# Linear attention in chunks of 64 tokens of two batches, with its products in quarter and eighth parts of the TensorE array

## The chip, the cores and the metric

The kernel runs on one core of a Trainium2 chip. The metric is the device time of one execution in microseconds. The kernel before takes 512.79 us (median of 3 runs, 512.62 to 513.18).

## The reference

The program computes a linear attention with a decaying state and feeds its output, token by token, to a feed-forward layer with a cosine gate. Cut to what is computed:

```python
# r, k, v: (4 batches, 8 heads, 768 tokens, 48), w, u: (8, 48)
for t in range(S):
    cur = einsum('bhd,bhe->bhde', u * k[t], v[t])
    y[t] = einsum('bhd,bhde->bhe', r[t], state + cur)
    state = w[..., None] * state + einsum('bhd,bhe->bhde', k[t], v[t])
x = y.transpose(0, 2, 1, 3).reshape(3072, 384)
h = x @ w_in                      # (384, 2048)
out = (h * cos(h)) @ w_out        # (2048, 384)
```

The two weights are given in 64-bit floats, everything else in 32-bit floats; the output is float32.

## The kernel before, in words

**Attention** is cut into 24 chunks of 128 tokens of one batch (`chunk(i)`: batch `i % 4`, part `i // 4` of its 768 tokens). Within a chunk, k and r are brought into a form with the 48 entries of a head along the partitions (two heads, `j` = 0 and 1, at partitions 0 to 47 and 64 to 111; four such pairs `p`), scaled with the decay. Then four products follow on TensorE (PE), all in float32:

- the scores, `mm_a` (L819): k by r for 8 heads, 128x128 each. Head `j` uses one half of the array's rows and writes to a PSUM bank of its own;
- `mm_x` (L840): r by the state before the chunk (`zt`), 12 pieces of 32 output rows each, in four column parts of the array;
- `mm_x2` (L853): the masked scores `A` by v, 16 pieces of 32 output rows, added to the same bank;
- `mm_z` (L875): k by v, the chunk's own contribution to the state, 48x48 for each head.

Between them ScalarE (ACT) writes a diagonal matrix into `A` (L809, the term with u) and VectorE (DVE) copies the scores above the diagonal over it (L826, `copy_predicated`). After `mm_z` DVE adds the contribution to the state `zc` and multiplies by the decay (L932, L933; L930 for a batch's first chunk), and ACT spreads it to `zt` (L868). The result x is split into a high and a low part (L914 on ACT, L919 on DVE).

The first 12 chunks have k and r transposed on PE (L730). The other 12 ("late") load k and r in a staged form and have them transposed by DVE (L738) and scaled by GpSimd (POOL, L743).

**The feed-forward part** takes blocks of 3 chunks (384 tokens). A step is 9 matmuls for h (L316: high and low parts, three products of three slices), the gate on ACT and DVE (qi L327, rest L330, cos L333, gate L1030, gh L1033, gl L1036) and 9 matmuls for the output (L322). Weights come as 64-bit words (`raw`) and are turned into high and low parts on ACT, DVE and POOL.

**Order.** A planner in the program itself (`Plan`) takes every piece of work as an operation with an engine, a due time, a cost and the buffers that it needs, plays the program many times with changed due times, keeps the best order and emits the instructions in that order. Each engine then works through its own list in order. A buffer (`Buf`) is bound to a tile of a ring by the planner. The 8 PSUM banks are such tiles: three for the output sums (`B_ACC`), two or three for h, and three for late attention chunks (`B_ATT`: two for scores, then x, then state). All chunk loads are issued by SyncE (SP).

## Time and profile before

| | us |
|---|---|
| median of 3 runs | 512.79 |
| profiled execution, its own time | 512.26 |
| its span, first to last instruction | 510.5 |
| PE busy in the span | 501.5 (98%) |
| DVE, ACT, POOL busy | 381.0, 331.0, 177.1 |

A row of a group reads: line, engine, operation, output and inputs, shape, count; then busy time and the mean duration in ns of one; then idle time before it and what ended it. A timeline row is start, length, and then the instruction with the count of records that were merged. Busy time of PE is the union of overlapping records.

### The profile page before, as it was taken

What the parts mean: (1) busy time and instruction counts of PE and PEld (TensorE: products, weight loads), DVE (VectorE), ACT (ScalarE), POOL (GpSimd) and SP (SyncE); (2) the same over time, 40 slices, a digit from 0 to 9 for tenths busy, and PEclk for the clock granted to TensorE, in tenths of its full rate; (3) what the DMA queues carried; (4) which work ended last, traced back from release to release, by engine and by line L of the source; (5) the groups of instructions that cost most, each with busy time, mean ns of one, the idle gap of its engine ahead of it and who ended that gap; (6) DMA issues with size and microseconds to landing.
All of it is one profiled execution on the core that took longest, in us unless ns stands there. A gap on an engine that the chain in (4) does not pass through costs nothing.

```text
span 510.5 us, 11742 instructions
## 1 busy us (share of the span) xinstructions
PE 501.5 (98%) x4389; PEld 480.0 (94%) x4389; DVE 381.0 (75%) x773; ACT 331.0 (65%) x833; POOL 177.1 (35%) x184
## 2 busy tenths in 40 slices
PE   8999999999999999999999999999999999999995
PEld 5788899999999999999999999999999999999995
DVE  6898999888888875576777777777777767756553
ACT  2989987767667756556657465575665765655453
POOL 6777422445454451242426224224044041300000
PEclk9999999999999999999999999999999999999999
DMA  8999226586666593524676736446455465200001
GB/s 137 179 179 190 79 86 218 152 167 156 157 140 131 127 180 44 76 65 67 160 146 151 159 99 167 111 156 152 105 130 140 142 170 114 89 16 33 1 1 49
DMA packets 114975, 61.56 MB, mean 121 GB/s; under 512 B 78433, under 2 KB 110818, under 8 KB 114914
## 3 DMA queue, kind: packets, MB, share of 16 engines
q1 hardware_dynamic: 109586, 53.50, 42.7%
q0 software_dynamic: 5184, 7.08, 9.9%
q8 instruction: 35, 0.57, 0.5%
q14 instruction: 26, 0.21, 0.2%
q10 hardware_dynamic: 144, 0.20, 0.1%
HBM read 48.96 MB, written 11.80 MB: 119 GB/s over the span
## 4 chain that ended last, share of the span: by engine, by line
PE 94%; DMA 2%; DVE 1%; ACT 1%; issue 1%; POOL 0%; SPq 0%; DVEq 0%; POOLq 0%; ACTq 0%
PE bank L322 41%; PE bank L316 39%; PE bank L819 4%; PE bank L853 4%; PE bank L840 3%; PE bank L875 2%; PE bank L730 1%; DMA v<-in_v_dram 1%; DMA k<-in_k_dram 1%; ACT A L809 1%; PE bank L1094 0%; DVE pq L440 0%; POOL f L765 0%; DVE a L800 0%; DVE rq L447 0%
## 5 line engine op out<-in xcount | busy, mean ns | idle before, releaser
L322 PE MATMUL bank<-w_out_hi,gh 128*128 128x384 f32 x384 | 131.9, 344 | 0.0
L322 PE MATMUL bank<-w_out_hi,gl 128*128 128x384 f32 x384 | 129.8, 338 | 0.0
L316 PE MATMUL bank<-xh,w_in_lo 128*128 128x384 f32 x384 | 129.7, 338 | 0.0
L322 PE MATMUL bank<-w_out_lo,gh 128*128 128x384 f32 x384 | 129.5, 337 | 0.0
L316 PE MATMUL bank<-xh,w_in_hi 128*128 128x384 f32 x384 | 129.1, 336 | 0.0
L316 PE MATMUL bank<-xl,w_in_hi 128*128 128x384 f32 x384 | 128.8, 335 | 0.0
L330 DVE SCALAR_TENSOR_TENSOR f<-bank,qi 128x384 f32<-128x384 f32 (+1 forms) x132 | 71.4, 543 | 47.0 <-ACT qi L327 46.5
L327 ACT ACTIVATE qi<-bank 128x384 int32<-128x384 f32 (+1 forms) x132 | 62.8, 479 | 57.7 <-PE bank L316 57.0
L1033 ACT CAST gh<-f 128x384 fp32r<-128x384 f32 (+1 forms) x132 | 65.7, 500 | 48.9 <-DVE f L1030 46.9
L1030 DVE TENSOR_TENSOR f<-bank,f 128x384 f32<-128x384 f32 (+1 forms) x132 | 71.2, 542 | 32.5 <-ACT f L333 30.3
L1036 DVE TENSOR_TENSOR gl<-f,gh 128x384 fp32r<-128x384 f32 (+1 forms) x132 | 80.7, 613 | 19.6 <-ACT gh L1033 19.1
L333 ACT ACTIVATE f<-f 128x384 f32<-128x384 f32 (+1 forms) x132 | 67.3, 513 | 41.6 <-DVE f L330 40.8
L322 PEld LDWEIGHTS bank<-w_out_hi,gh 128*128 128x128 f32 x384 | 72.0, 188 | 3.0 <-issue 0.8
L316 PEld LDWEIGHTS bank<-xh,w_in_lo 128*128 128x128 f32 x384 | 72.2, 188 | 0.3 <-DVE w_in_lo L631 0.3
L316 PEld LDWEIGHTS bank<-xh,w_in_hi 128*128 128x128 f32 x384 | 72.2, 188 | 0.3 <-issue 0.2
L316 PEld LDWEIGHTS bank<-xl,w_in_hi 128*128 128x128 f32 x384 | 72.1, 188 | 0.0
L322 PEld LDWEIGHTS bank<-w_out_hi,gl 128*128 128x128 f32 x384 | 72.1, 188 | 0.0
L322 PEld LDWEIGHTS bank<-w_out_lo,gh 128*128 128x128 f32 x384 | 72.0, 188 | 0.0
L809 ACT ACTIVATE A<-ident,a 128x128 f32<-128x128 f32 x192 | 59.6, 391 | 4.9 <-DVE a L800 4.8
L743 POOL TENSOR_TENSOR kT<-kT,decT_k 112x512 f32<-112x512 f32 x12 | 15.6, 1301 | 129.3 <-DVE kT L738 74.4
L621 POOL TENSOR_TENSOR f<-f,raw 128x384 int32<-128x384 int32 x32 | 36.7, 1148 | 60.8 <-DVE f L610 31.7
L1078 POOL DMA_DIRECT2D out_dram<-f x36 | 32.7, 1012 | 40.6 <-DVE f L1030 17.2
(88 smaller groups left out, 589.5 us busy)
## 6 DMA issues: line engine op xcount, KB each, us to landing
raw<-in_moe_w_in_dram SPq DMA_DIRECT2D x32, 384.0 KB, 3.2
raw<-in_moe_w_out_dram SPq DMA_DIRECT2D x32, 384.0 KB, 3.2
out_dram<-f POOLq DMA_DIRECT2D x36, 192.0 KB, 4.5
k<-in_k_dram SPq DMA_DIRECT2D x24, 192.0 KB, 4.2
v<-in_v_dram SPq DMA_DIRECT2D x24, 192.0 KB, 5.1
raw<-in_k_dram SPq DMA_DIRECT2D x47, 96.0 KB, 3.1
raw<-in_r_dram SPq DMA_DIRECT2D x47, 96.0 KB, 2.1
out_dram<-f SPq DMA_DIRECT2D x23, 192.0 KB, 1.9
```

Of the source, the lines that this page charges most:

```text
L316: nc.tensor.matmul(ph, a, b_, start=(i == 0), stop=(i == len(mm) - 1))
L322: nc.tensor.matmul(acc, a[:, ts], b_[:, f, :], start=(first and i == 0), stop=(last and i == 2))
L327: nc.scalar.activation(qi, ph, AF.Copy, scale=INV_2PI, bias=0.25)
L330: nc.vector.scalar_tensor_tensor(q, ph, INV_2PI, qi, op0=ALU.mult, op1=ALU.subtract)
L333: nc.scalar.activation(q, q, AF.Sin, scale=TWO_PI, bias=0.5 * math.pi)
L621: lambda: nc.gpsimd.tensor_tensor(ai(), ai(), cn(), op=ALU.add),
L809: nc.scalar.activation(A[j]()[:, p, :], ident, AF.Copy, scale=ab()[:, h : h + 1])
L819: nc.tensor.matmul(cube(Ap[j])[:, p, :], kT()[ps, p, :], rT()[ps, p, :], start=True, stop=True)
L1030: nc.vector.tensor_tensor(g()[:, cs], ph()[:, cs], q()[:, cs], op=ALU.mult)
L1033: nc.scalar.copy(gh()[:, cs], g()[:, cs])
L1036: nc.vector.tensor_tensor(gl()[:, cs], g()[:, cs], f32(gh())[:, cs], op=ALU.subtract)
L1078: nc.gpsimd.dma_start(dst, ob(), accum_op=ALU.add)
```

## The change

A chunk is now 64 tokens of two batches (`m = i % 2` is the pair of batches, `c = i // 2` one of 12 parts): the first batch's tokens stand at partitions 0 to 63 of the natural layout, the other's at 64 to 127. There are still 24 chunks of 128 tokens, and blocks of the feed-forward part still have 3.

- Scores: 16 matmuls of 64x64 instead of 8 of 128x128; head `j` picks the rows, batch `b` the columns of the array. The square blocks between the two batches are no longer computed. `A`, the diagonals and the masks have 64 columns for each head instead of 128.
- State: 16 matmuls with 64 rows each, directly behind the scores in the same operation (the first two chunks have them apart); only a batch pair's last chunk has none, so 22 chunks have a state and 22 read one (20 and 20 before). `zc` and `zt` hold two batches.
- `mm_x`: 24 matmuls of 32x64 instead of 12 of 32x128. `mm_x2`: 32 matmuls of 32x64 with 64 rows instead of 16 of 32x128 with 128 rows, written so that eight in a row are in eight different parts of the array.
- PSUM: scores with state, and x, each take a pair of neighbouring banks, one bank for each half of the array's rows. The planner knows pairs (`parts`). Late chunks have one pair (banks 5 and 6) for both; h has three banks throughout.
- Each load of a chunk is two DMA issues of 64 partitions, and eight instead of four for the staged ones.

The core of the diff:

```diff
+        pair = [Tile(bank_all[:, i : i + 2], bank[i : i + 2]) for i in range(7)]
+        B_ACC, B_H, B_ATT = bank[0:3], bank[3:5] + bank[7:8], bank[5:8]
+        P_ATT = pair[5:6]
+        P_EARLY = [pair[5], pair[6], pair[3], pair[0]]
...
-            b, c = i % B, i // B
+            m, c = i % NM, i // NM
...
-            Ap = [Buf(bk) for _ in range(2)]
+            sp = Buf(bp)
-            xp = Buf(bk)
-            zp = Buf(bk)
+            xp = Buf(bp)
+            half = [slice(b * CT, (b + 1) * CT) for b in range(2)]
...
+                    for b in range(2):
+                        nc.sync.dma_start(
+                            buf()[half[b], :, 0:D], src[2 * m + b, :, ts, :].rearrange("h t d -> t h d")
+                        )
...
-                        nc.scalar.activation(A[j]()[:, p, :], ident, AF.Copy, scale=ab()[:, h : h + 1])
+                        nc.scalar.activation(A[j]()[:, p, :], ident2, AF.Copy, scale=ab()[:, h : h + 1])
...
+            def mm_z():
+                z = state_in()
+                for p in range(NP):
+                    for j in range(2):
+                        for b in range(2):
+                            h = 2 * p + j
+                            nc.tensor.matmul(
+                                z[j * DP : j * DP + DP, b, p, :],
+                                kb()[half[b], h, :],
+                                vb()[half[b], h, 0:D],
+                                start=True,
+                                stop=True,
+                            )
...
-                        nc.tensor.matmul(cube(Ap[j])[:, p, :], kT()[ps, p, :], rT()[ps, p, :], start=True, stop=True)
+                        for b in range(2):
+                            nc.tensor.matmul(
+                                score(j)[half[b], p, :],
+                                kT()[ps, p, half[b]],
+                                rT()[ps, p, half[b]],
+                                start=True,
+                                stop=True,
+                            )
+                if more and not first:
+                    mm_z()
...
-                    A[j](), upper[:, None, :].to_broadcast([P, NP, C]), cube(Ap[j])
+                    A[j](), upper[:, None, 0:CT].to_broadcast([P, NP, CT]), score(j)
...
+                rounds = (
+                    ((0, 0), (1, 0), (2, 0), (3, 0)),
+                    ((4, 0), (1, 1), (6, 0), (7, 0)),
+                    ((4, 1), (5, 0), (10, 0), (7, 1)),
+                    ((8, 0), (9, 0), (10, 1), (11, 0)),
+                )
+                for group in rounds:
+                    for b in range(2):
+                        for g, n in group:
...
-                    return lambda: nc.scalar.copy(zb()[ps, :, j * D : (j + 1) * D], zc[b][ps])
+                    return lambda: nc.scalar.copy(zb()[ps, :, :, j * D : (j + 1) * D], zc[m][ps])
...
-                        nc.vector.tensor_tensor(zc[b], z, zc[b], op=ALU.add)
-                        nc.vector.tensor_tensor(zc[b], zc[b], w_c, op=ALU.mult)
+                        nc.vector.tensor_tensor(zc[m], z, zc[m], op=ALU.add)
+                        nc.vector.tensor_tensor(zc[m], zc[m], w_c, op=ALU.mult)
```

The order on PE around the first late chunk, before. The rows with `w_in` and `w_out` belong to the feed-forward part; `rT`, `kT` are the scores, `zt` is r by the state, `A` is the masked scores by v, and `v`, `k` the state:

```order
L322 MATMUL bank_76<-w_out_lo,gh_113 128x384
L819 MATMUL bank_83<-rT_96,kT_94 128x128
L819 MATMUL bank_82<-rT_96,kT_94 128x128
...
L322 MATMUL bank_78<-w_out_hi,gh_114 128x384
...
L840 MATMUL bank_83<-rT_96,zt_124 32x128 x12
L853 MATMUL bank_83<-A_99,v_89 32x128 x2
...
L875 MATMUL bank_82<-v_89,k_86 48x48 x8
L322 MATMUL bank_78<-w_out_hi,gh_112 128x384
```

The same place now:

```order
L336 MATMUL bank<-w_out_lo,gh_106 128x384
L876 MATMUL bank<-rT_89,kT_87 64x64 x16
L863 MATMUL bank<-v_82,k_79 64x48 x16
L336 MATMUL bank<-w_out_hi,gh_107 128x384
...
L923 MATMUL bank<-rT_89,zt_115 32x64 x24
L948 MATMUL bank<-A_92,v_82 32x64 x2
L948 MATMUL bank<-A_93,v_82 32x64
L948 MATMUL bank<-A_92,v_82 32x64 x3
...
L336 MATMUL bank<-w_out_hi,gh_105 128x384
```

The state has moved from the second block to the first, and each attention product has twice as many matmuls of half the columns. Eighteen big matmuls stand between the two blocks in both.

DVE between the two blocks of a late chunk, before (`COPY_PREDICATED` is the mask, `zc` the state, `gl` the last piece of a feed-forward step, `xl` the chunk's result):

```order
L826 COPY_PREDICATED A_101<-upper,bank_81 128x512
L826 COPY_PREDICATED A_102<-upper,bank_82 128x512
L1030 TENSOR_TENSOR f_108<-bank_80,f_108 128x384
L1036 TENSOR_TENSOR gl_116<-f_108,gh_113 128x384
L330 SCALAR_TENSOR_TENSOR f_110<-bank_79,qi_111 128x384
L532 SCALAR_TENSOR_TENSOR f_105,warm<-f_106 128x384
L1030 TENSOR_TENSOR f_110<-bank_79,f_110 128x384
L932 TENSOR_TENSOR zc_123<-bank_81,zc_123 112x192
L933 TENSOR_TENSOR zc_123<-zc_123,pq 112x192
L1036 TENSOR_TENSOR gl_117<-f_110,gh_114 128x384
```

The same place now:

```order
L1000 TENSOR_TENSOR zc_114<-bank,zc_114 112x384
L1001 TENSOR_TENSOR zc_114<-zc_114,pq 112x384
L901 COPY_PREDICATED A_94<-upper,bank 128x256
L901 COPY_PREDICATED A_95<-upper,bank 128x256
L1104 TENSOR_TENSOR gl_108<-f_102,gh_105 128x384
L1098 TENSOR_TENSOR f_101<-bank,f_101 128x384
L344 SCALAR_TENSOR_TENSOR f_103<-bank,qi_104 128x384
L559 SCALAR_TENSOR_TENSOR f_100,warm<-f_99 128x384
L1104 TENSOR_TENSOR gl_109<-f_101,gh_106 128x384
```

The state's two instructions have moved ahead of the masks, in front of the next gl, and have twice the columns; the masks have half.

More of the change, by code (lines that the diff above doesn't have):

```diff
@@ L95, in _free_at @@
     def _free_at(tile):
-        if tile.owner is None:
-            return 0.0
-        if any(o.end is None for o in tile.owner.users):
-            return None
-        return max(o.end + o.lat for o in tile.owner.users)
+        t = 0.0
+        for x in tile.parts:
+            if x.owner is None:
+                continue
+            if any(o.end is None for o in x.owner.users):
+                return None
+            t = max(t, max(o.end + o.lat for o in x.owner.users))
+        return t
     def _ready(self, o):
@@ L110, in _ready @@
             for tl in b.tiles:
-                if id(tl) in taken:
+                if any(id(x) in taken for x in tl.parts):
                     continue
@@ L117, in _ready @@
                 return None
-            taken.add(id(best[1]))
+            taken.update(id(x) for x in best[1].parts)
             picks.append((b, best[1]))
@@ L136, in latest @@
             for b in o.bufs:
-                owners = tiles.setdefault(b.tile, [])
-                if not owners or owners[-1][0] is not b:
-                    if all(b is not x for x, _ in owners):
-                        owners.append((b, o))
+                for part in b.tile.parts:
+                    owners = tiles.setdefault(part, [])
+                    if not owners or owners[-1][0] is not b:
+                        if all(b is not x for x, _ in owners):
+                            owners.append((b, o))
         for owners in tiles.values():
@@ L202, in one_pass @@
                 for tl in b.tiles:
-                    tl.owner = None
+                    for x in tl.parts:
+                        x.owner = None
         nxt, left = {}, {}
@@ L234, in one_pass @@
             for b, tl in picks:
-                b.tile, tl.owner = tl, b
+                b.tile = tl
+                for x in tl.parts:
+                    x.owner = b
             o.gap = t - free[o.eng]
@@ L822, in chunk @@
+                if more and not first:
+                    mm_z()
+            with_z = more and not first
+            last_A[0] = o_A = op(
+                PE,
+                due - 1.7,
+                0.7 + (0.45 if with_z else 0.0),
+                mm_a,
+                [e_k, e_r] + ([o_kd, l_v] if with_z else []),
+                [kT, rT, sp] + ([kb, vb] if with_z else []),
+                lat=0.3,
+            )
             first_A.append(o_A)
+            zo = o_A
             def mask(j):
@@ L845, in mm_x2 @@
-            def mm_x2():
-                x = xv()
-                for g in range(NK * 4):
-                    p, s = divmod(g, 3)
-                    gs = slice(G * (g % 4), G * (g % 4) + G)
-                    parts = {0: ((0, 0),), 1: ((0, G), (1, D)), 2: ((1, DP + 16),)}[s]
-                    for n, (j, at) in enumerate(parts):
-                        nc.tensor.matmul(
-                            x[gs, g // 4, :],
-                            vb().rearrange("q h d -> q (h d)")[:, p * 2 * DP + at : p * 2 * DP + at + G],
-                            A[j]()[:, p, :],
-                            start=(not c and g < 4 and n == 0),
-                            stop=(n == len(parts) - 1),
-                            skip_group_check=True,
-                        )
+                x = xm()
@@ new lines, in mm_x @@
+                for kk in range(NK):
+                    for b in range(2):
+                        for g in range(4 * kk, 4 * kk + 4):
+                            p, s = divmod(g, 3)
+                            gs = slice(G * (g % 4), G * (g % 4) + G)
+                            nc.tensor.matmul(
+                                x[gs, b, kk, :],
+                                zb()[:, b, p, G * s : G * s + G],
+                                rT()[0:KP, p, half[b]],
+                                start=(kk == 0),
+                                stop=False,
+                                skip_group_check=True,
+                            )
@@ new lines, in mm_x2 @@
+            def mm_x2():
+                x = xm()
+                rounds = (
[4 rows of a table added]
+                )
+                for group in rounds:
+                    for b in range(2):
+                        for g, n in group:
+                            p, s = divmod(g, 3)
+                            gs = slice(G * (g % 4), G * (g % 4) + G)
+                            parts = {0: ((0, 0),), 1: ((0, G), (1, D)), 2: ((1, DP + 16),)}[s]
+                            j, at = parts[n]
+                            nc.tensor.matmul(
+                                x[gs, b, g // 4, :],
+                                vb().rearrange("q h d -> q (h d)")[half[b], p * 2 * DP + at : p * 2 * DP + at + G],
+                                A[j]()[half[b], p, :],
+                                start=(not c and g < 4 and n == 0),
+                                stop=(n == len(parts) - 1),
+                                skip_group_check=True,
+                            )
```

180 lines of the change are left out of this document (85 added, 95 removed).

## The prediction

> **What bounds the kernel now.** I read the page's shares of the engines first, then the chain of waits, then busy time by stretch.
>
> ```profile
> PE 501.5 (98%) x4389; PEld 480.0 (94%) x4389; DVE 381.0 (75%) x773; ACT 331.0 (65%) x833; POOL 177.1 (35%) x184
> PE 94%; DMA 2%; DVE 1%; ACT 1%; issue 1%; POOL 0%; SPq 0%; DVEq 0%; POOLq 0%; ACTq 0%
> 0.00:10.70 10.70, 8.31 (x52) 5.63 (x52) 6.62 (x21) 1.97 (x3) 6.57 (x22) 1.00 0.75 132
> 10.70:63.40 52.70, 51.37 (x1013) 43.74 (x1012) 47.45 (x90) 48.74 (x145) 37.74 (x37) 1.00 0.91 155
> 63.40:505.20 441.80, 441.80 (x3329) 430.60 (x3326) 326.86 (x664) 279.81 (x685) 132.78 (x126) 1.00 0.49 116
> 505.20:510.50 5.30, 0.02 (x1) 0.00 (x0) 0.08 (x1) 0.48 (x1) 0.00 (x0) 0.91 0.32 116
> ```
>
> The first two lines say that TensorE is the bound. The rows by stretch (length, then busy us of PE, PEld, DVE, ACT, POOL; clock; DMA share; GB/s) say where it has company. From 63.4 us on PE has no idle time at all, and every nanosecond taken off it there comes off the end. From 10.7 to 63.4 us, where the first 12 attention chunks run, PE has 51.4 of 52.7 us, but ACT has 48.7, DVE 47.5 and the DMA engines 0.91: time taken off PE there soon uncovers another engine.
>
> ```profile
> L819 PE MATMUL bank<-rT,kT 48*128 48x128 f32 x384 | 27.6, 284 | 0.3 <-ACT kT L790 0.2
> L853 PE MATMUL bank<-A,v 128*32 128x128 f32 x768 | 26.8, 275 | 0.9 <-DVE A L826 0.8
> L840 PE MATMUL bank<-rT,zt 112*32 112x128 f32 x480 | 17.2, 277 | 0.0
> L875 PE MATMUL bank<-v,k 128*48 128x48 f32 x320 | 11.1, 212 | 0.2 <-DMA v<-in_v_dram 0.2
> ```
>
> These are attention's own products: scores (L819), masked scores by v (L853), r by the state (L840), the state (L875). Together about 83 us of PE; each matmul of the program is two records here.
>
> **The price of one record.** The next rows (start, length) show two chunks of the early stage back to back and then one chunk of the late stage, between matmuls of the feed-forward part.
>
> ```profile
> 58.84 2.06 PE L819 MATMUL bank<-rT,kT 48*128 48x128 f32 x32
> 60.82 0.93 PE L875 MATMUL bank<-v,k 128*48 128x48 f32 x32
> 61.68 0.86 PE L840 MATMUL bank<-rT,zt 112*32 112x128 f32 x24
> 62.36 1.08 PE L853 MATMUL bank<-A,v 128*32 128x128 f32 x32
> 212.84 0.34 PE L322 MATMUL bank<-w_out_lo,gh 128*128 128x384 f32 x1
> 213.10 1.16 PE L819 MATMUL bank<-rT,kT 48*128 48x128 f32 x16
> 214.19 0.44 PE L322 MATMUL bank<-w_out_hi,gh 128*128 128x384 f32 x1
> 214.48 0.34 PE L322 MATMUL bank<-w_out_hi,gl 128*128 128x384 f32 x1
> 217.09 0.34 PE L322 MATMUL bank<-w_out_hi,gl 128*128 128x384 f32 x1
> 217.27 0.34 PE L322 MATMUL bank<-w_out_lo,gh 128*128 128x384 f32 x1
> 217.54 0.86 PE L840 MATMUL bank<-rT,zt 112*32 112x128 f32 x24
> 218.22 1.08 PE L853 MATMUL bank<-A,v 128*32 128x128 f32 x32
> 219.23 0.56 PE L875 MATMUL bank<-v,k 128*48 128x48 f32 x16
> 219.72 0.45 PE L322 MATMUL bank<-w_out_hi,gh 128*128 128x384 f32 x1
> 220.01 0.34 PE L322 MATMUL bank<-w_out_hi,gl 128*128 128x384 f32 x1
> ```
>
> Sixteen score records more (32 against 16) make the row 0.90 us longer: 0.056 us each, though one lasts 284 ns by its group's row. So they overlap, and by position (two heads in two halves of the array's rows) two run at a time: a pair every 112 ns. Sixteen state records more cost 0.37 us (0.93 less 0.56): a pair every 46 ns, two at a time in two halves of the columns. In L853 four parts of 32 columns run at a time: 0.81 us from first to last start (1.08 less one record's 0.27) over 7 steps of four, about 112 ns with a longer first one, so 109. From 128 and 48 streamed columns (112 and 46 ns) follows a rule for one step: 6 ns and 0.83 ns per column. **At 64 columns a step costs 59 ns.**
>
> A block between the big matmuls pays for the change of shape too. 217.09 to 217.27 is the usual 0.18 us between big ones; 212.84 to 213.10 is 0.26, so 0.09 to enter; the step out of a block costs about 0.09 more, and the first big one behind is 0.29 ahead of the next, 0.11 too much. First steps in a block are longer as well: 0.10 us for 128 stationary columns (16 score records of 8 steps would be 0.89 between entry and exit, and the block's 1.35 us less entry and exit leaves 1.0), in proportion about 0.05 for 64.
>
> **The change on PE, late chunks** (12 of them behind 63.4 us). Now, the score block costs 214.19 - 212.84 - 0.18 + 0.11 = 1.29 us, the other block 219.72 - 217.27 - 0.18 + 0.11 = 2.38, or 1.89 without the state (0.49 from 219.23 to 219.72). Eight chunks have a state and four have none: 8 x 3.67 + 4 x 3.18 = 42.1 us. Afterwards:
> - Scores: 16 matmuls, 32 records, four at a time in 64x64 parts: 8 steps x 59 = 0.47 us (0.89 now).
> - State: 32 records in the same shape right behind the scores, 48 streamed but 64 stationary columns: 8 steps of 46 to 59, I take 52: 0.42 (0.37 now).
> - r by state: 48 records, four at a time: 12 x 59 = 0.71 (0.65 now: 6 x 109).
> - Masked scores by v: 64 records, eight at a time in 64x32 parts: 8 x 59 = 0.47 (0.87 now).
> - Entries, exits, first steps: 0.09 + 0.09 + 0.11 + 0.05 for the score block, 0.09 + 0.09 + 0.11 + 0.02 and one more change of shape (0.09 + 0.02) for the other: 0.76.
>
> That is 2.83 us for each of 10 chunks and 2.41 for the last two, which have no state: 33.1. **Late gain 9.0 us.**
>
> No row shows parts split by rows and by columns at once. The bounds: two at a time for scores and state and four for L853, as the rows have it, which adds 0.47 + 0.42 + 0.47 = 1.36 us per chunk; or the full 4 and 8. I take the full, because halves of rows (scores) and quarters of columns (L853) each overlap completely, and because the row parts write to different banks in both kernels. The Trainium skill, page "TensorE: Matmul & The Clock Gate", section "Part 3: Packing small matmuls — row/col tiling", states that row and column parts combine; nothing of this case shows it yet.
>
> **The early 12 chunks.** On PE each gains the same: scores and state 0.37 us between them, L853 0.40, fewer changes of shape 0.15, r by state loses 0.06; ten chunks instead of eight need r by state (two pairs of batches, so only the first two chunks have no state to read): +1.4. 12 x 0.86 - 1.4 = 8.9 us off. Two of three feed-forward steps (18 matmuls, 3.2 us) now stand behind this stage, too. So PE would need 51.4 - 8.9 - 3.2 = 39.3 us; the others decide.
>
> ```profile
> L826 DVE COPY_PREDICATED A<-upper,bank 128x512 f32<-128x512 int32 x24 | 17.2, 739 | 3.3 <-ACT A L809 1.9 <-PE bank L819 1.1
> L755 DVE TENSOR_TENSOR rT<-bank,decT_r 112x512 f32<-112x512 f32 x11 | 7.5, 678 | 0.0
> L933 DVE TENSOR_TENSOR zc<-zc,pq 112x192 f32<-112x192 f32 x6 | 4.6, 769 | 0.2
> L932 DVE TENSOR_TENSOR zc<-bank,zc 112x192 f32<-112x192 f32 x6 | 2.1, 345 | 0.0
> L809 ACT ACTIVATE A<-ident,a 128x128 f32<-128x128 f32 x96 | 29.6, 392 | 3.6 <-DVE a L800 3.5
> L790 ACT COPY kT<-bank 112x512 f32<-112x512 f32 x10 | 5.8, 578 | 1.4 <-issue 1.2 <-ACT zt L868 0.2
> L868 ACT COPY zt<-zc 48x192 f32<-48x192 f32 x16 | 5.6, 349 | 0.2
> SPq L672 <- PE bank L875: 6.7, 7, 1.6
> q1 hardware_dynamic: 26559, 6.34, 107.3%
> ```
>
> (Groups of that stretch; then what SP's queue waited for until 64 us; the last row is the DMA queue from 10.7 to 46 us.) **DVE**: L932 and L755 differ by 320 columns and 333 ns, 1.04 ns each. The masks lose 256 of 512 columns, 0.27 of 0.72 us: 17.2 us to 10.8. But the state's two instructions double to 384 columns, 0.345 to 0.55 and 0.77 to some 1.05 us, for nine chunks and two first ones instead of six and four: about +7.4. The feed-forward steps that leave take 2.7 (two of L330 and L1030 and one gl at 0.55 each). DVE: 47.5 to 45.8 us. **ACT**: L868 and L790 give 0.7 ns per column; the diagonals lose 64 columns each, 96 x 0.045 = 4.3 of 29.6 us; zt doubles to about 0.48 us, 20 instead of 16: +4.1; the feed-forward -3.3. ACT: 48.7 to 45.2. **DMA** is at 107% of its engines until 46 us; the chunks' bytes stay, each load now two issues of 64 partitions. 36 loads of 0.197 MB at 6.34 MB in 35.3 us are 39 us, so the last chunk's data come at 46 to 48 us and its end can't be before about 55.
>
> So the stage ends when DVE has done 45.8 us, at the 90% that it reaches now (50.9 us) or at nearly all (46). I take 95%, 48.2 us: it ends at 58.9 instead of 63.4 us, **-4.5** (-1.8 to -7). Behind it stand 18 more big matmuls (+3.2) and a last chunk's block 0.3 cheaper.
>
> **Costed at nothing**: on late chunks DVE has the state (0.55 us twice) and the masks (0.45 twice) between the score block and the other one, since both wait for one pair of banks; PE does 18 big matmuls (3.15 us) there, so about 1 us is spare. If gl of the step behind the masks came late, PE would stand some 0.5 us per chunk, 5 us in all. Twice the issues on SP have room, for SP's queue stands waiting for buffers (6.7 us for L875 alone). A start with the second half of a load later by one issue: up to +0.5, within the range.
>
> **The sum**: 510.5 - 9.0 - 4.5 + 3.2 - 0.3 = 499.9 us of span. The profiled execution took 512.26 with that span of 510.5, and the median is 512.79: +2.3. **502.2 us.** Its own range is 498 to 507 (the early stage's bounds, a stall of part of the late chunks).
>
> **Rivals.**
> 1. *PE's whole gain is kept early* (DVE and ACT fill up): 512.8 - 9.0 - 8.9 - 0.3 = 494.6. For: DVE and ACT have only some 46 us each. Against: ACT and DMA, all close to their limits together.
> 2. *L853 runs four at a time, not eight*: +0.47 x 12 late (5.6) and about 2 us early, where DVE covers most: 510. Against: the steps within a group of four follow each other fast.
> 3. *Row and column parts never overlap with each other*, the slower case: +1.36 us per chunk, 16.3 late and on PE early 16.3 less 6 that DVE covers: 502.2 + 26, about 528. It decides from an extra 0.45 us per chunk.
> 4. *Each record costs a fixed time at issue.* Records go from 1,952 to 4,064, and the densest row here is one per 23 ns (L875). At 23 ns a chunk's 176 records take 4.05 instead of 2.07 us: +2.0 x 24 less early cover: about 541. The Trainium skill's page "TensorE: Matmul & The Clock Gate", section "Wait — 56ns, not 53.3ns?", states a floor of about 25 ns from start to start. L875's 23 ns is already below that, so the trace does not hold with it for different parts.
>
> **How the numbers follow.** Forecast 0.62; rival 1 0.12; rival 2 0.13 (0.11 of it faster); rival 3 0.08; rival 4 0.03; no change for a cause not named 0.02. A difference under 0.2% (about 1 us) can't be told from none. Faster 0.85, same 0.04, slower 0.11. The range, 494.5 to 511, leaves out rivals 3 and 4 and some edge of rival 1.
>
> **What would show it.** A late score-and-state block should take 1.1 to 1.3 us between big matmuls and the other 1.5 to 1.7; steps of 64 columns some 59 ns; no idle PE behind the early stage; the early stage should end near 59 us with PE under 90% busy and DVE over 92%. Blocks of 1.9 us and more would be rival 3 or 4; idle PE at r by state, a late DVE chain.

## The result, and the profile after

The changed kernel takes 693.04 us (median of 4 runs, 690.57 to 694.85) beside 512.98 us for the kernel before on the same chip: 1.351 times as long, interval 1.346 to 1.355. The forecast was 502.2 us. The profiled execution took 692.22 us with a span of 690.5.

From the page of the changed kernel, the busy time and the chain by engine:

```profile
PE 548.9 (79%) x6501; PEld 513.7 (74%) x6501; DVE 377.6 (55%) x778; ACT 327.2 (47%) x837; POOL 194.3 (28%) x186
...
DMA 42%; PE 33%; DVE 6%; issue 6%; POOL 5%; SPq 4%; ACT 3%; POOLq 0%; ACTq 0%; DVEq 0%
```

Its busy time by stretch (length, then busy us of PE, PEld, DVE, ACT, POOL, granted clock, DMA share, GB/s):

```profile
10.70:63.40 52.70, 39.23 (x1444) 32.61 (x1442) 30.00 (x59) 32.91 (x104) 30.07 (x31) 0.84 0.66 129
63.40:94.50 31.10, 25.55 (x721) 23.21 (x722) 24.51 (x49) 21.07 (x58) 8.51 (x9) 0.95 0.31 78
94.50:674.20 579.70, 475.91 (x4295) 452.19 (x4293) 317.54 (x651) 270.43 (x672) 148.64 (x125) 0.91 0.39 88
```

PE went from 98% busy to 79%, and the chain from 94% PE to 42% DMA. The reader should see two losses. By 94.5 us the changed kernel has started as many big feed-forward matmuls (61) as the kernel before had by 71.1 us: 23.4 us lost early. The rest then takes 579.7 us where it took 434.1 (71.1 to 505.2): 145.6 us lost. Of these, 103.8 us are idle time of PE; the other 41.8 us are longer busy time (475.9 us against 434.1), at a granted clock of 0.91. So the large loss lies outside the products: PE waits, and its clock is lower.

Who holds PE there? Two rows of the changed kernel's waits (us in total, times, longest):

```profile
PE bank L336 <- DVE gl L1104: 41.9, 19, 7.4
DVE f L344 <- DMA out_dram<-f: 80.6, 19, 9.8
```

Its DMA view, a queue (packets, MB, share of the engines) and an issue (count, size, median us from issue to landing):

```profile
q0 software_dynamic: 37440, 7.34, 8.9%
...
out_dram<-f POOLq DMA_DIRECT2D x36, 192.0 KB, 13.8
```

The same two rows of the kernel before:

```profile
q0 software_dynamic: 5184, 7.08, 9.9%
...
out_dram<-f POOLq DMA_DIRECT2D x36, 192.0 KB, 4.5
```

The same 36 accumulating stores of 192 KB take 13.8 us from issue to landing instead of 4.5, in seven times as many packets. The 4,608 packets that hold one output row each are there in both kernels, and their times add up to 713 us, against 799 before; new are 32,256 packets of 8 bytes, 267 us in all. So the packets together did not take three times as long: fewer of them ran at a time. Tiles of the ring `f` (six) stay held until then; DVE's first gate instruction (L344) waits 80.6 us in 19 pieces for one of them, and PE waits behind DVE (41.9 us for the last piece of a step alone).

The cause stands in the last lines of the change, which neither the description of the change nor the prediction spoke of. The output rows of a chunk are no longer one range of 128 rows:

```diff
-                    row = (jc % B) * S + (jc // B) * C
-                    dst = out[row : row + C, :]
+                    m, c = jc % NM, jc // NM
+                    dst = out.rearrange("(b s) d -> b s d", b=B)[2 * m : 2 * m + 2, c * CT : (c + 1) * CT, :]
```

The destination's outermost dimension is now 2 (batches), not 128 (rows). In the trace the packets of one plain store from SP that runs alone go about 2 at a time (2.1 on average, 3.9 us a store); before they went 13 at a time (0.65 us). The Trainium skill, page "DMA: Bandwidth & Descriptors", section "Rules for kernel authors", states just this: the slowest dimension of the access patterns sets how many of the 16 engines a DMA uses, and an outermost one of size c below 16 confines the whole transfer to at most c of them. The trace agrees, with 2.

The products themselves did become shorter. Two late blocks of the changed kernel (start, length, instruction, merged records):

```profile
329.61 0.34 PE L336 MATMUL bank<-w_out_lo,gh 128*128 128x384 f32 x1
329.88 0.69 PE L876 MATMUL bank<-rT,kT 48*64 48x64 f32 x32
330.40 0.63 PE L863 MATMUL bank<-v,k 64*64 64x48 f32 x32
330.96 0.44 PE L336 MATMUL bank<-w_out_hi,gh 128*128 128x384 f32 x1
...
334.03 0.34 PE L336 MATMUL bank<-w_out_lo,gh 128*128 128x384 f32 x1
334.29 0.88 PE L923 MATMUL bank<-rT,zt 112*32 112x64 f32 x48
335.10 0.86 PE L948 MATMUL bank<-A,v 64*32 64x64 f32 x64
335.89 0.44 PE L336 MATMUL bank<-w_out_hi,gh 128*128 128x384 f32 x1
```

With the prediction's own arithmetic (start to start, less 0.18, plus 0.11) the first block is 1.28 us and the second 1.79: 3.07 us for a chunk, where it was 3.67 and 2.83 was forecast.

### The profile page after: what moved, and what is told of

Read it like the earlier page. It is cut to its first block, busy times and chain, and to the rows that moved or that the text cites. A ratio compares the mean times of both kernels' runs of the same rounds, so it can differ in the third digit from the quotient of the medians.

```text
span 690.5 us, 16304 instructions
## 1 busy us (share of the span) xinstructions
PE 548.9 (79%) x6501; PEld 513.7 (74%) x6501; DVE 377.6 (55%) x778; ACT 327.2 (47%) x837; POOL 194.3 (28%) x186
## 4 chain that ended last, share of the span: by engine, by line
DMA 42%; PE 33%; DVE 6%; issue 6%; POOL 5%; SPq 4%; ACT 3%; POOLq 0%; ACTq 0%; DVEq 0%
DMA out_dram<-f 33%; PE bank L330 13%; PE bank L336 11%; DMA f<-in_r_dram 3%; PE bank L923 2%; PE bank L948 2%; DMA raw<-in_moe_w_in_dram 2%; SPq L730 2%; SPq L702 1%; PE bank L863 1%; DMA v<-in_v_dram 1%; PE bank L767 1%; DMA raw<-in_r_dram 1%; DVE gl L1104 1%; PE bank L876 1%
## 5 line engine op out<-in xcount | busy, mean ns | idle before, releaser
L336 PE MATMUL bank<-w_out_hi,gh 128*128 128x384 f32 x384 | 138.9, 362 | 47.3 <-ACT f L1131 21.7
L336 PE MATMUL bank<-w_out_hi,gl 128*128 128x384 f32 x384 | 138.1, 360 | 41.9 <-DVE gl L1104 41.9
L330 PE MATMUL bank<-xh,w_in_hi 128*128 128x384 f32 x384 | 138.9, 362 | 4.0 <-ACT w_in_hi L653 4.0
L330 PE MATMUL bank<-xh,w_in_lo 128*128 128x384 f32 x384 | 138.1, 360 | 0.0
L330 PE MATMUL bank<-xl,w_in_hi 128*128 128x384 f32 x384 | 137.7, 359 | 0.0
L344 DVE SCALAR_TENSOR_TENSOR f<-bank,qi 128x384 f32<-128x384 f32 (+1 forms) x132 | 70.7, 538 | 95.2 <-DMA out_dram<-f 80.6
L1104 DVE TENSOR_TENSOR gl<-f,gh 128x384 fp32r<-128x384 f32 (+1 forms) x132 | 82.1, 624 | 27.6 <-ACT gh L1101 26.5
L330 PEld LDWEIGHTS bank<-xh,w_in_hi 128*128 128x128 f32 x384 | 79.2, 206 | 5.0 <-ACT w_in_hi L653 4.5
L330 PEld LDWEIGHTS bank<-xl,w_in_hi 128*128 128x128 f32 x384 | 79.3, 207 | 0.0
L330 PEld LDWEIGHTS bank<-xh,w_in_lo 128*128 128x128 f32 x384 | 78.9, 205 | 0.4 <-DVE w_in_lo L658 0.4
L1146 POOL DMA_DIRECT2D out_dram<-f x36 | 51.1, 1700 | 42.9 <-ACT f L1131 14.4
L846 ACT ACTIVATE A<-ident,a 128x64 f32<-128x64 f32 x192 | 49.5, 337 | 4.3 <-DVE a L837 4.0
## 6 DMA issues: line engine op xcount, KB each, us to landing
out_dram<-f POOLq DMA_DIRECT2D x36, 192.0 KB, 13.8
```

Of the source, the lines that this page charges most:

```text
L330: nc.tensor.matmul(ph, a, b_, start=(i == 0), stop=(i == len(mm) - 1))
L336: nc.tensor.matmul(acc, a[:, ts], b_[:, f, :], start=(first and i == 0), stop=(last and i == 2))
L344: nc.vector.scalar_tensor_tensor(q, ph, INV_2PI, qi, op0=ALU.mult, op1=ALU.subtract)
L846: nc.scalar.activation(A[j]()[:, p, :], ident2, AF.Copy, scale=ab()[:, h : h + 1])
L1104: nc.vector.tensor_tensor(gl()[:, cs], g()[:, cs], f32(gh())[:, cs], op=ALU.subtract)
L1146: nc.gpsimd.dma_start(dst, ob(), accum_op=ALU.add)
```

## The experiments

In what follows "t61" is the time at which the 61st big matmul (128x384) starts, a mark for the end of the early stage that is the same piece of work in all kernels: 71.1 us in the kernel before, 94.5 in the changed one. "The rest" runs from there to the last big matmul's end: 434.1 and 579.7 us.

### Is it the store?

First the changed kernel with each output store as two transfers of 64 rows:

```diff
-                            nc.gpsimd.dma_start(dst, ob(), accum_op=ALU.add)
+                        for b in range(2):
+                            part = ob()[b * CT : (b + 1) * CT]
...
+                                nc.gpsimd.dma_start(dst[b], part, accum_op=ALU.add)
```

> The changed kernel with one edit: each output store is two DMAs of 64 rows instead of one DMA whose outermost dimension has the length 2. Theory A (a store of that shape is served by two DMA engines only, so it lands late and holds the f tiles that the gate needs): stores land as fast as in the kernel before, TensorE's idle time behind the early stage goes, and what stays is the early stage's own loss (it ended near 84 us instead of 63): 520 to 535 us. Rival B (the late loss is the attention's own: one pair of banks, VectorE's longer state, the lower clock): the time stays above 600 us, with the same idle time at the same places.

Measured: **553.92 us** (549.29 to 557.0), 1.080 times the kernel before (1.076 to 1.084). So 139 of the 180 us were the store's shape. The time is above the 520 to 535 us that were expected; what is left of the loss is taken up below.

Second the other way round, the kernel before with the changed kernel's destination and nothing else:

```diff
-                    row = (jc % B) * S + (jc // B) * C
-                    dst = out[row : row + C, :]
+                    m_, c_ = jc % 2, jc // 2
+                    dst = out.rearrange("(b s) d -> b s d", b=B)[2 * m_ : 2 * m_ + 2, c_ * 64 : (c_ + 1) * 64, :]
```

> The kernel before with one edit: its output stores take the changed kernel's shape (two halves of 64 rows of two batches), so rows land at places of the output where they do not belong; nothing else differs. Theory A: 620 to 690 us, VectorE and ScalarE waiting for f tiles that stores still hold. Rival B: 513 us within 3.

Measured: **645.63 us**, ratio 1.256 (1.253 to 1.259): 132 us from the store alone, with attention untouched. From its waits:

```profile
DVE f L330 <- DMA out_dram<-f: 62.8, 15, 8.9
```

and from its DMA view:

```profile
q0 software_dynamic: 37440, 7.34, 9.6%
...
out_dram<-f POOLq DMA_DIRECT2D x36, 192.0 KB, 13.6
```

The same wait at the same instruction (L330 here, L344 in the changed kernel), the same packets, the same 13.6 us. The two runs bracket the main cause from both sides.

### What remains: 41 us of the new form itself

In the run with two stores t61 is 92.0 us (20.9 late) and the rest 449.5 us (15.4 long), although each late chunk is about 0.5 us shorter on PE. Its stretches, and three of the four windows before t61 in which its granted clock was 0.50 (27.3 us in all; the kernel before has none there):

```profile
10.70:63.40 52.70, 41.03 (x1446) 34.93 (x1447) 30.38 (x60) 33.24 (x104) 32.11 (x32) 0.78 0.68 132
...
92.00:541.50 449.50, 435.83 (x4295) 421.86 (x4293) 325.18 (x651) 271.54 (x672) 158.94 (x161) 0.99 0.50 113
...
12.40:19.20 6.80, 6.80 (x201) 6.05 (x201) 3.73 (x8) 4.23 (x16) 5.42 (x6) 0.50 0.74 136
36.30:46.50 10.20, 8.41 (x194) 7.13 (x191) 5.39 (x12) 4.80 (x16) 4.94 (x5) 0.50 0.64 133
60.20:67.00 6.80, 5.54 (x80) 5.18 (x76) 2.82 (x6) 0.99 (x2) 3.12 (x4) 0.50 0.55 119
```

In the early stage no engine is near its limit: PE 41.0 of 52.7 us and at a clock of 0.78, ACT 33.2, DVE 30.4, DMA 0.68. The longest waits of PE up to 90 us, in total, are these:

```profile
PE bank L863 <- issue: 4.7, 3, 2.0
...
PEld bank L863 <- issue: 5.3, 4, 2.1
PEld bank L948 <- issue: 3.9, 7, 1.2
```

A piece of its timeline:

```profile
32.40 0.69 PE L876 MATMUL bank<-rT,kT 48*64 48x64 f32 x32
32.91 0.28 PE L863 MATMUL bank<-v,k 64*64 64x48 f32 x5
35.18 0.67 PE L863 MATMUL bank<-v,k 64*64 64x48 f32 x27 [1.99 <-issue]
```

The state's products stop after 5 of 32 records, for 2 us, with nothing that they wait for ("issue"). Counting all of PE's instructions from the start (matmuls, weight loads and the semaphore instructions between them), the breaks in the middle of a product come at numbers 1474, 1730, 2242, 2498, 2754, 3010, 3778 and 4034: all multiples of 256 apart. They are 0.5 to 2.0 us long and 8.4 us in all. The kernel before has no such break.

**Is it SP?** One candidate was SP, which issues twice as many loads. The early v loads went to ACT's queue:

```diff
-            l_v = op(SP, due - 5.0, 1.2, load(vb, v), ahead, [vb], lat=2.6, line=ln)
+            l_v = op(
+                SP if late else ACT, due - 5.0, 1.2, load(vb, v, nc.sync if late else nc.scalar), ahead, [vb], lat=2.6, line=ln
+            )
```

> As e1_two_stores, but the first 12 chunks' v loads are issued by ScalarE instead of SyncE. Theory C (SyncE's issue time, 0.6 us for each 64-partition DMA and so 3.6 us and more a chunk, sets the pace of the early stage): the early stage and the whole are 6 to 15 us shorter than e1_two_stores. Rival D (TensorE's pauses at every 256th instruction of its list, while new code comes in, set it): within 3 us of e1_two_stores, with as many pauses.

Measured: 555.6 to 558.6 us in three runs and 564.4 in a fourth, t61 at 95.4. No gain; relieving SP of a third of its early chunk loads is not what the stage needs.

**Is it the traffic of the loads?** The early chunks loaded 4 of 8 heads (the other four stay zero):

```diff
-                            buf()[half[b], :, 0:D], src[2 * m + b, :, ts, :].rearrange("h t d -> t h d")
+                            buf()[half[b], 0:NH, 0:D], src[2 * m + b, 0:NH, ts, :].rearrange("h t d -> t h d")
```

> As e1_two_stores, but the first 12 chunks load only four of eight heads of k, r and v (the rest of the tiles is set to zero once), so half of the early data is not moved and the output is not the reference's; the count of DMA issues is the same. Theory C: if an issue costs the same 0.6 us, the early stage ends within 3 us of e1_two_stores. Rival D with its cause in the data traffic (code has to queue behind data on the DMA engines): the pauses of TensorE at every 256th instruction go from about 9 to at most 3 and the stage is 6 to 12 us shorter. If the pauses stay, the traffic is not their cause.

Measured: 549.95 us (one run), t61 at 89.6, and breaks at six of the same eight numbers. Half the bytes take away few of the breaks, and move the end by 2.4 us.

**Is it a planner that believes old costs?** The planner was told the issue times that the trace shows:

```diff
-                l_ks = op(SP, due - 6.2, 2.2, load_s(ks, k), ahead, [ks], lat=4.0, line=ln)
+                l_ks = op(SP, due - 6.2, 4.2, load_s(ks, k), ahead, [ks], lat=4.0, line=ln)
...
-            l_k = op(SP, due - 5.2, 1.2, load(kb, k), ahead, [kb], lat=2.6, line=ln)
+            l_k = op(SP, due - 5.2, 1.4, load(kb, k), ahead, [kb], lat=2.6, line=ln)
...
-                        0.6 if f0 == 0 else 1.1,
+                        1.2 if f0 == 0 else 2.8,
```

> As e1_two_stores (553.9 us), but the planner is told what the DMA issues took in that run: 4.2 us for the eight issues of a staged load (2.2 before), 1.4 for a load's two (1.2), 1.2 and 2.8 for a store's two (0.6 and 1.1). Theory E (behind the early stage TensorE's idle 15 us are late loads of chunks, planned too short): idle time there goes from 15 us to under 5, 540 to 545 us. Rival (those waits come from DVE and GpSimd, not from the planned issue times): within 4 us of 553.9.

Measured: 543.9 us, ratio 1.060 (1.055 to 1.064), 10 us better, though PE's idle time behind t61 fell only from 13.7 to 10.4 us, not to under 5. And t61 is 91.3 us; of the 4.3 us between the two profiled runs 4.1 lie in the rest (445.4 us instead of 449.5). The early stage keeps its loss.

**Is it the number of PE's instructions?** r by the state was left out in the ten early chunks that have it, 960 matmuls and weight loads fewer:

```diff
-                if c:
+                if c and late:
                     mm_x()
```

> As e1_two_stores, but the early chunks leave out r by the state (24 matmuls, 96 TensorE instructions with the weight loads, in each of 10 chunks; the output is not the reference's). Theory F (the early stage is as long as it takes to bring in TensorE's code, some 62 instructions per us): 960 instructions less, the stage 12 to 17 us shorter. Rival (SyncE's issues or VectorE set its end): within 5 us of e1_two_stores. 0.8 us of TensorE's own time in each of 10 chunks would be 8 us if TensorE's array were the limit.

Measured: 541.71 us, ratio 1.056 (1.053 to 1.058): 12.2 us less, t61 at 82.1. The stage is 9.9 us shorter, less than the 12 to 17 of the theory, and r by the state also takes 0.81 us of the array each time, 8 us in all. (What it reads, `zt`, is no rival: no wait of PE up to 90 us in the run with two stores names it.) So a later run put other work of the array in its place, with 8 instructions where 96 were (r by the state stays left out there):

```diff
             def mm_x():
+                if not late:
+                    for _ in range(4):
+                        nc.tensor.matmul(
+                            xp()[:, 0, 0 : 2 * P], warm, warm[:, None, :].to_broadcast([P, 2, P]), start=True, stop=True
+                        )
+                    return
```

> Edit: as the run without r by state in the early stage (ten early chunks), but in its place PE gets four products of 128 by 256 columns in bf16 per chunk, 213 ns each, 0.85 us against the 0.81 us that r by state took undisturbed; 8 instructions where 96 were. Theory F (what the early stage loses by r by state is the number of its instructions, which PE has to fetch): as without it, 541 to 545 us. Rival (it is PE's own array time, 0.81 us ten times over): as with it, 551 to 556 us.

Measured: **541.91 us**, ratio 1.056 (1.053 to 1.059), t61 at 83.5. Two rows of it:

```profile
30.59 0.60 PE L919 MATMUL bank<-warm 128*128 128x256 bf16 x4
31.12 0.86 PE L954 MATMUL bank<-A,v 64*32 64x64 f32 x64
```

The four products took 0.53 us start to start, not the 0.85 of the expectation: 213 ns is what one takes at a granted clock of 0.50 (at 28 us in this run), 109 what it takes otherwise. So the array did about 5.3 us more work than without them, and the time is the same within what the two can be told apart; compared with the run that has r by the state, the array lost 2.8 us and the kernel gained 12. So most of the gain is paid for the number of instructions: t61 falls by 9.9 us for 960 of them, and by 8.5 for the 880 taken out here, about 10 ns each. Part of that goes by way of the clock: the time at 0.50 before t61 is 13.7 us in both runs, not 27.3.

This explains about half of the 20.9 us. The new form has 2,112 instructions more than the old one by t61 (4,417 against 2,305), and 10 ns for each would be 21 us, but that is only an estimate, and the trace of the run without r by the state does not bear it out. There t61 is still 11.0 us late, with 1,152 instructions more than the old form, the breaks are 1.6 us in all, and PE's longest wait is another one:

```profile
PE bank L767 <- POOL k L810: 4.8, 1, 4.8
```

What holds these other 11 us was not tested.

Why would a number of instructions cost time? The queue that brings them, in the page of the kernel before:

```profile
q8 instruction: 35, 0.57, 0.5%
```

and of the changed one:

```profile
q8 instruction: 52, 0.85, 0.5%
```

0.57 MB is 65 bytes for each of the 8,778 matmuls and weight loads, 0.85 MB is 65 bytes for each of 13,002, and one packet is 16 KB: 256 instructions, the distance of the breaks. The Trainium skill, page "Runtime: NRT & Kernel Launch", section "Instruction fetch mechanics", states refills in blocks of 16 KiB, 256 instructions, and calls the cost of crossing such a boundary mostly hidden. The spacing agrees; "mostly hidden" does not hold here, where 256 instructions of the dense early stage pass in 3 to 6 us and a break is 0.5 to 2.0 us. The trace also has the time of each packet. In the run with two stores each of the eight breaks ends 1.1 to 1.6 us after the packet before it had been moved; over the nine runs that have such breaks (of more than 0.2 us, inside one product, where the matmul waits for nothing) it is so for all 54, at 1.0 to 1.7 us, and all 54 lie on the same grid of 256. So PE goes on when code has come in. That is read from traces; no run changed the fetching alone.

### Do the small parts of the array pay by themselves?

The kernel before, with its 128-column products cut into two of 64 moving columns, no change of tokens, loads or stores:

```diff
-                    for j in range(2):
+                    for e in (slice(0, 64), slice(64, 128)):
+                        for j in range(2):
...
+                            nc.tensor.matmul(cube(Ap[j])[:, p, e], kT()[ps, p, :], rT()[ps, p, e], start=True, stop=True)
```

> The kernel before, with scores, r by the state and masked scores by v each issued as two matmuls of 64 columns in place of one of 128 (the same parts of the array, the same columns in all, twice the instructions). Nothing else is changed. Theory F: the early stage's 3,900 TensorE instructions would need some 63 us at 62 per us, so pauses at every 256th instruction appear there, and it ends 8 to 14 us later; with 6 ns more for each step (4 us in all): 522 to 530 us. Rival (no limit by code): 515 to 519 us, no such pauses.

Measured: 540.55 us, ratio 1.053 (1.051 to 1.055), above what was expected. The pauses that were expected are there, with the old tokens, loads and stores: at PE's instructions 2242, 2498 and 3010, three of the numbers above, 0.4, 1.4 and 0.5 us long. This is the second of them:

```profile
55.30 0.61 PE L820 MATMUL bank<-rT,kT 48*128 48x64 f32 x8
57.29 0.44 PE L820 MATMUL bank<-rT,kT 48*128 48x64 f32 x4 [1.38 <-issue]
```

They are the smaller part. Behind t61 (86.9 us) PE is 100% busy and the rest is 12.6 us longer, so that is array time. A late score block took 2.20 us between big matmuls where it took 1.36 with half as many instructions, and the other block 2.67 instead of 2.46. In the scores a step with 128 stationary columns does not get shorter with 64 moving ones: it stays near 110 ns. In r by the state, with 32 stationary columns, it does: 12 steps took 0.69 us here, 6 took 0.68. The 64-token chunk is needed for a 64-column step to be worth half; and with 48 moving and 64 stationary columns (the state) a step takes 58 ns, not 46: the larger of the two numbers of columns sets it.

The one product that missed its price is L948, 0.79 us for 64 records, with the step out of the block, where 0.47 was forecast. Eight-record steps within it: 10, 7, 7 and 9.5 ns for each record of the first half, a jump at the 33rd (18 ns on average over those eight), then 8, 8 and 14. To tell a limit on the rate from the order of the second half, the late chunks issued the whole product twice (the second adds the same terms again):

```diff
                 mm_x2()
+                if late:
+                    mm_x2()
```

> Edit: after with two stores, but in the late chunks the 32 products of masked scores by v (64 array records) are issued a second time right behind the first, so that records 65 to 128 repeat records 1 to 64. In the first pass records 1 to 32 start every 7 ns on average and 33 to 64 every 12. Theory H (instructions are taken in faster than array time only while a store of those read ahead lasts, and after it one per about 12 ns): all records of the second pass come every 11 to 13 ns, and it adds 0.75 us or more to each block. Rival (the second half's row and column parts overlap less by their own order): the second pass repeats 7 and 12 ns and adds about 0.6 us.

Measured: 559.87 us (one run); the second pass adds 0.63 us to an undisturbed block (2.49 us between big matmuls instead of 1.86), 9.8 ns a record. Two undisturbed rows and two disturbed ones:

```profile
268.22 1.49 PE L948 MATMUL bank<-A,v 64*32 64x64 f32 x128
269.63 0.44 PE L336 MATMUL bank<-w_out_hi,gh 128*128 128x384 f32 x1
...
244.76 0.59 PE L948 MATMUL bank<-A,v 64*32 64x64 f32 x35
246.85 0.31 PE L948 MATMUL bank<-A,v 64*32 64x64 f32 x6 [1.50 <-issue]
```

The theory of a store that runs empty expected 0.75 us or more and falls; the rival's 0.6 us is what came, though the two halves of the second pass are nearly alike (9.5 and 11.0 ns a record), not 7 and 12. Records in different parts of the array start 8 to 11 ns apart, averaged over 32 of them, and this does not get worse up to 128; what makes the jump at the 33rd stays open. The last two rows show something else: four of the twelve late blocks have a break of 1.4 to 1.7 us inside this product. Counted as above, they come at PE's instructions 6594, 8642, 10690 and 12738: exactly eight times 256 apart, and a multiple of 256 behind the early ones. Twice the small products late bring the early stage's breaks into the late blocks.

### The late half alone

If the early stage is what the new form spoils, the first 12 chunks should keep the old form and only the last 12 take the new one. Core of the edit (early chunks by the old function, then the decay tables halved once):

```diff
+            if i == XS:
+                last_zm[:] = [last_z[0:2], last_z[2:4]]
...
+                            f_ = (pq if up != y else rq)[:, :, 11:12].to_broadcast([P, NP, CT])
+                            v_ = t[:, :, y * CT : (y + 1) * CT]
+                            nc.vector.tensor_tensor(v_, v_, f_, op=ALU.mult)
...
-            x_ready.setdefault(n, []).extend(chunk(i, due, xb[i]))
+            x_ready.setdefault(n, []).extend((chunk if i >= XS else chunk_early)(i, due, xb[i]))
```

> Edit: the first 12 chunks are computed as in the kernel before (128 tokens of one batch, tokens 0 to 383 of each), the last 12 in the new form (64 tokens of two batches); between them the decay tables are halved once by two DVE products, four transposes and a copy. Rows of the early chunks are stored in one transfer of 128 rows, rows of the late ones in two of 64, and the planner has the DMA costs of the run with real issue costs. Theory G (the new form loses in the early stage alone and pays in the late blocks): the 61st big matmul falls at 71 us as before, and twelve late chunks gain 3.67 less 3.08 us each, 7 us, of the 434 us behind it: 504 to 508 us, faster than before. Rival (late, the 64-row loads cost SP twice the issues, and PE waits for them there whatever the early stage did, 10 us in the run with real issue costs, with another 5 for the half clock after such waits): 71 + 445 + 7 us around it, 518 to 526 us.

Measured: 521.73 us (521.56 to 523.36), ratio 1.016 (1.014 to 1.018). t61 is back at 72.9 us, as expected, but the rest is 442.6 us and PE idle in it for 8.4 us: the rival. What SP does for one late chunk in this run, and below it in the kernel before (start, length):

```profile
375.38 4.61 SPq L1019 DMA_DIRECT2D raw<-in_k_dram  x8
380.08 4.74 SPq L1019 DMA_DIRECT2D raw<-in_r_dram  x8
384.93 1.30 SPq L991 DMA_DIRECT2D k<-in_k_dram  x2
386.33 1.27 SPq L1013 DMA_DIRECT2D f<-in_r_dram  x2
387.69 1.28 SPq L991 DMA_DIRECT2D v<-in_v_dram  x2
```

```profile
378.58 1.76 SPq L693 DMA_DIRECT2D raw<-in_k_dram  x4
382.90 1.74 SPq L693 DMA_DIRECT2D raw<-in_r_dram  x4
384.74 0.38 SPq L672 DMA_DIRECT2D k<-in_k_dram  x1
385.22 0.53 SPq L688 DMA_DIRECT2D f<-in_r_dram  x1
385.80 0.57 SPq L672 DMA_DIRECT2D v<-in_v_dram  x1
```

13.2 us of issuing instead of 5.0 for the same bytes: an issue of half the partitions is not shorter (0.58 to 0.65 us each, against 0.38 to 0.57). The first of them starts only behind the scores of the chunk before, by a rule in the kernel (`ahead`), and chunks follow each other every 18 to 25 us. So k is scaled late and the mask is late: PE waits 0.6 us at the state for the one and 2.8 us at r by the state for the other, and 4.7 us more in the feed-forward part.

That rule was then taken out, and, as a control, taken out of the kernel before as well:

```diff
-            ahead = [last_A[0]] if late else []
+            ahead = []
```

> Edit: the run with the late part alone, and the loads of a late chunk are no longer held back until the scores of the chunk before it are placed (the list of operations they stand after is empty), so that the planner may issue them as soon as their tiles are free. Theory I (what is left of the loss is SP: the five loads of a late pair cost it 13.2 us of issuing, 4.6 + 4.7 + three of 1.3, out of some 20 us between pairs, and they may start only behind the scores of the pair before): without that rule most of PE's 8.4 us of idle and of the 5 us at half clock behind it go, 507 to 513 us, level with the kernel before or up to 1.2% faster. Rival (the raw tiles that the range checks share, or DVE's late masks, hold the chunks as well): 517 to 523 us.

> Edit: the kernel before with that one rule taken out as well, and nothing else, as the control of the run above: whether the rule costs the old form anything. Theory I: PE had no idle time behind its 61st big matmul in the kernel before, so nothing can be gained: 511 to 515 us. Rival (the rule costs any form): below 510 us.

Measured: 514.35 us (12 runs), ratio 1.0018 (1.0002 to 1.0033), and for the control 513.92 us, ratio 1.0003 (0.9988 to 1.0018). The stretch behind t61 in the run with the rule:

```profile
72.90:515.50 442.60, 434.18 (x4299) 421.61 (x4297) 319.24 (x652) 274.80 (x672) 131.69 (x126) 0.99 0.51 116
```

and without it:

```profile
73.20:506.90 433.70, 431.06 (x4315) 420.89 (x4313) 325.79 (x652) 274.64 (x673) 129.77 (x124) 1.00 0.51 117
```

The idle time falls from 8.4 to 2.6 us, and 7.4 us of the total come back, a little less than expected (507 to 513 us). The rule costs the old form nothing. The new form in the late half is then level with the kernel before and no better. In the profiled runs its undisturbed blocks are 6.2 us shorter in all. Against that stand two blocks with a wait for the mask (1.4 and 1.2 us), 3.1 us longer together; slower steps between big matmuls, 1.6 us; 0.9 us of attention work that falls behind t61; and a t61 that is 2.1 us later. A version that beats the kernel before was not found.

## Why the prediction was wrong, point by point

The forecast was 191 us short. The profiled run with two stores was the fastest of its four, 4.6 us below their median; with that, the miss divides into 139 for the store, 22.5 for the early stage (t61 at 92.0; 71.1 - 4.5 + 3.2 - 0.3 = 69.5 was forecast), 24.4 for the rest (449.5 against 434.1 - 9.0) and that 4.6.

1. **The step that failed is one that the sum does not contain.** Its parts were PE, the early stage and "Costed at nothing"; the output store's new destination, the last lines of the change, appears in none. It costs 132 us in the old kernel and 139 in the new one. A row for it was at hand: stores landing in 4.5 us, and a destination with an outermost dimension of 2. No rival named it either, so the slower cases (528 and 541 us) had the sign right by other mechanisms.
2. **"Twice the issues on SP have room, for SP's queue stands waiting for buffers."** False for the late chunks: 13.2 us of issuing instead of 5.0, of the 18 to 25 that the rule leaves. It was argued from waits of the early stage, and there moving a third of these loads off SP gained nothing.
3. **"So the stage ends when DVE has done 45.8 us", -4.5 us.** DVE did not set it: 30 us busy in that stretch, DMA 0.68. The stage became 20.9 us longer. It was treated as a sum of busy times, and the number of PE's instructions, which nearly doubles up to t61, was given no price beyond the array's. Rival 4 came nearest, a price for each record, but placed it in every block at 23 ns; late blocks don't show it. In the early stage 880 to 960 matmuls and weight loads fewer moved t61 by 8.5 to 9.9 us, about 10 ns each, with the breaks and the half clock that go with them; what makes the other 11 us of the 20.9 stays open.
4. **Late gain 9.0 us: mechanism right, size off.** Row and column parts do run at once (rival 3 is out: a chunk costs 0.24 us more than forecast, where 0.45 was to decide for it; between big matmuls the first block takes 1.35 us and the second 1.86, just above the 1.1 to 1.3 and 1.5 to 1.7 of the forecast). Start to start, each with the step into what follows: scores 0.52 us (0.47 forecast), state 0.56 (0.42), r by state 0.81 (0.71), masked scores by v 0.79 (0.47); entries and exits came out smaller. Ten chunks at 3.07 us and two without a state at 2.62 are 35.9 us where 42.1 stood: 6.2 us. The mis-sized terms are L853's "eight at a time" (10 ns a record from the first start to the last, not 7; rival 2 would be 0.94 us) and the state's step, for which 52 was taken between 46 and 59 and 58 came.
5. **"No idle PE behind the early stage"** was the check that the result broke first: 103.8 us with the store as it is, 13.7 with two stores.
6. **DVE's late chain** was priced well and did not become the bound by its length:

```profile
L901 DVE COPY_PREDICATED A<-upper,bank 128x256 f32<-128x256 int32 x24 | 9.8, 442 | 0.4 <-ACT A L846 0.3
L1001 DVE TENSOR_TENSOR zc<-zc,pq 112x384 f32<-112x384 f32 x10 | 5.6, 558 | 0.3
L1000 DVE TENSOR_TENSOR zc<-bank,zc 112x384 f32<-112x384 f32 x10 | 5.5, 552 | 2.2 <-PE bank L863 2.2
```

0.44 for a mask and 0.55 and 0.56 for the state, as forecast (0.45 and twice 0.55).

## What to carry to other kernels

Read the diff to its last line and list every DMA whose access pattern changes shape, with its outermost dimension and its number of issues; a store that stays the same size in bytes can become six times as slow. When a change multiplies instructions in a stretch that is already dense, price the count itself as well as the array time, and look for breaks at even distances in the list of instructions. A gain on the bounding engine is kept only if what feeds it has room in the same stage, so read the room in that stage, not in another one.

## What the runs showed of the hardware that was not expected

- A store whose destination has an outermost dimension of 2 had about 2 packets under way at a time instead of 13: 3.9 us instead of 0.65 for 192 KB from SP. The accumulating ones took 13.8 us instead of 4.5 from issue to landing, with 896 packets of 8 bytes added to each.
- PE breaks off for 0.5 to 2.0 us, in the middle of a product, at multiples of 256 instructions, where 256 of them pass in 3 to 6 us; each of 54 such breaks ended 1.0 to 1.7 us after a packet of 16 KB of code. Among the big matmuls of the late stage, where 256 take some 22 us, nothing shows.
- Windows of 10.2 and 6.8 us at a granted clock of 0.50 began about 1 us behind the end of breaks of 2.0 and 0.9 us; two other such windows of that stage followed no break.
- A DMA issue on SP took about 0.6 us with 64 partitions and 0.4 to 0.6 with 128, so halving the partitions saved no time of issue.
- In scores, state and r by the state a step took as long as the larger of its stationary and moving columns asked for: near 110 ns with 128 stationary and 64 moving, 58 with 64 and 48, 57 with 32 and 64.
- Records in eight different parts of the array started 8 to 11 ns apart, averaged over 32, and the rate held over 128 records.
